# The first weight half by two DMA queues, and one zeroing matmul in bf16 in place of fp32

## The chip, the cores and the metric

The kernel runs on one core of a Trainium2 chip. The metric is the device time of one execution in us, as the median of several runs; the profiled span is some 1.8 us shorter.

## The reference

```python
def _attn_ref(x, f_logit, lower_bound):          # x, f_logit: (4, 6080, 256)
    sig = 1.0 / (1.0 + np.exp(-f_logit))
    f = lower_bound + (1.0 - lower_bound) * sig
    i = 1.0 - f
    for t in range(S):                           # S = 6080
        h = f[:, t] * h + i[:, t] * x[:, t]
        y[:, t] = h
    return y

def _moe_ref(x, w_in, w_out):                    # x: y as (24320, 256)
    h = x @ w_in                                 # w_in (256, 2048), w_out (2048, 256), float64
    g = h - np.tanh(h)
    return g @ w_out
```

## The kernel before

The tokens go in one block of 256 and 47 of 512. The weights come as 64-bit numbers and are turned into fp32 on the chip, in seven steps on DVE and ScalarE (`ce` to `cw`). The order of all work is a hand-made list of words. The start of the opening's list:

```python
before = """
    K1.7 W.0 df.0 ce.0 cr.0 dx.0 cm.0 tf.0 cx.0 W.1 cs.0 tx.0 sg0.0 cb.0 K1.4
    sg1.0 df.1 v0.0 f0.0 cw.0 f1.0 v1.0 dx.1 ce.1 tf.1 sc1.0 cx.1 sc0.0 W.2 cr.1
    cm.1 tx.1 sg1.1 cb.1 sg0.1 cs.1 F.0.0.0 f0.1 v1.1 f1.1 dx.2 v0.1 K1.4 cw.1
    t.0.0.0 sc0.1 q.0.0.0 F.0.0.1 w.0.0.0 W.3 sc1.1 cr.2 K1.2 a.0.0.0 t.0.0.1
    F.1.0.0 ...          # cut
    ... m13.2 K
    a.1.3.1 P1.2.0 ...   # cut
"""
```

`W.n` loads weights (`W.0` and `W.1` are halves of 512 KB), `df.j` and `dx.j` load f_logit and x of block j, `tf.j` and `tx.j` transpose them on TensorE, `sg` is the sigmoid, `sc` the scan over time on DVE. `F.j.u.s` are the first-layer products of the first two blocks. `K1.n` are n filler matmuls on zeros that keep TensorE busy. From block 2 on another scheme is used, in which products add to a bank that holds older sums; for its first use that bank is zeroed, by the word `K`:

```python
def fetch_half(u, s, raw, queue):
    src = moe_w_in.rearrange("(p k) (s u f) -> s u p k f", k=KC, s=2, u=NU)
    queue.dma_start(out=raw.rearrange("p (k f) -> p k f", k=KC), in_=src[s, u])

def keep_busy(n):                       # the word K1
    for _ in range(n):
        nc.tensor.matmul(busy[:], lhsT=zeros.bitcast(BF16)[:, 0:P],
                         rhs=zeros.bitcast(BF16)[:, 0:TB], start=True, stop=True, ...)

def clear_B():                          # the word K, once
    bank = ps_b.tile([P, 2, HB], FP32, name="B", tag="B")
    nc.tensor.matmul(bank[:], lhsT=zeros[:, 0:P], rhs=zeros[:], start=True, stop=True, ...)
...
nc.scalar.dma_start(out=lb[:], in_=lower_bound.rearrange("(p k) -> p k", k=KC))
```

Here P = 128, TB = 512, HB = 256 and KC = 2. The whole opening up to the first product of block 1 (`F.1.0.0`) takes 17.5 us.

## Time and profile before

| | kernel before |
|---|---|
| time, 3 runs | 2331.93, 2332.53, 2333.46 us |
| profiled run | 2331.1 us, span 2329.3 us |
| TensorE / DVE / ScalarE busy | 100% / 91% / 77% |
| first weight half landed | 4.78 us |
| x of block 1 issued, landed | 3.84, 11.53 us |
| first product `F.0.0.0` | 12.70 us |

The lines themselves stand in the prediction.

### The profile page before, as it was taken

The page shows a single profiled execution, that of the slowest core. Times are in us where ns is not written, and L with a number is a line of the kernel's source. Part 1 is how long each engine was busy: PE and PEld are TensorE (multiplying, and loading weights), DVE is VectorE, ACT ScalarE, POOL GpSimd, SP SyncE. Part 2 cuts the span into 40 slices and gives each one's busy share as a digit, 9 for nine tenths or more (in the row PEclk, how much of TensorE's full clock was granted, in tenths as well). Part 3 has the DMA queues.
Part 4 walks back from the last instruction along what each step waited for, and adds up shares of the span by engine and source line. Part 5 has one row for each costly group of instructions (what it writes and reads, how often), then busy time and mean ns, then how long its engine had stood idle before and what let it go on. Part 6 is the DMA issues. An engine that isn't in the chain of part 4 may idle for free.

```text
span 2329.3 us, 28648 instructions
## 1 busy us (share of the span) xinstructions
PE 2319.6 (100%) x10677; PEld 2025.2 (87%) x10677; DVE 2121.4 (91%) x2447; ACT 1801.1 (77%) x2686; POOL 0.7 (0%) x6
## 2 busy tenths in 40 slices
PE   9999999999999999999999999999999999999998
PEld 6888888888888888888888888888888888888887
DVE  8999899998999989999999999999899998999987
ACT  7677777777777777787777777777777777777775
POOL 0000000000000000000000000000000000000000
PEclk9999999999999999999999999999999999999999
DMA  6311211111111111112111121111211112111101
GB/s 172 64 24 32 42 37 28 28 35 39 37 28 28 37 36 37 28 28 42 32 37 28 28 45 28 37 28 28 46 29 36 28 28 46 31 33 28 28 10 29
DMA packets 296932, 85.05 MB, mean 37 GB/s; under 512 B 289872, under 2 KB 292688, under 8 KB 296784
## 3 DMA queue, kind: packets, MB, share of 16 engines
q1 hardware_dynamic: 296640, 83.14, 16.9%
q8 instruction: 85, 1.39, 0.2%
q14 instruction: 63, 0.52, 0.1%
q10 hardware_dynamic: 144, 0.00, 0.0%
HBM read 58.20 MB, written 24.90 MB: 36 GB/s over the span
## 4 chain that ended last, share of the span: by engine, by line
PE 99%; DMA 0%; SPq 0%; DVE 0%; issue 0%
PE A L383 27%; PE Qd L466 14%; PE Qa L466 14%; PE Qb L466 14%; PE D L383 14%; PE Qc L466 7%; PE B L383 7%; PE Qc L749 1%; PE Qb L749 1%; PE Qa L749 1%; PE A L682 1%; PE D L682 0%; PE Qd L682 0%; DMA xn<-in_x_dram 0%; PE B L682 0%; PE Qc L682 0%
## 5 line engine op out<-in xcount | busy, mean ns | idle before, releaser
L383 PE MATMUL A<-T,w_in 128*128 128x256 f32 x2208 | 558.8, 379 | 0.0
L383 PEld LDWEIGHTS A<-T,w_in 128*128 128x128 f32 x2208 | 419.5, 190 | 57.0
L427 DVE TENSOR_TENSOR h<-h,q 128x1024 f32<-128x1024 f32 x368 | 437.7, 1220 | 3.1
L421 DVE SCALAR_TENSOR_TENSOR q<-q,t 128x1024 f32<-128x1024 f32 x368 | 440.2, 1217 | 0.0
L414 ACT ACTIVATE q<-t 128x1024 f32<-128x1024 f32 x368 | 382.8, 1053 | 46.3 <-DVE h L427 43.4
L411 ACT ACTIVATE t<-h 128x1024 f32<-128x1024 f32 x368 | 388.7, 1057 | 3.1 <-DVE h L398 0.3
L432 ACT ACTIVATE junk<-t 128x1024 bf16<-128x1024 f32 x368 | 388.2, 1055 | 1.5
L446 DVE TENSOR_TENSOR Tg<-h 128x1024 f32<-128x1024 f32 x368 | 348.1, 946 | 6.4
L466 PE MATMUL Qb<-h,w_out 128*128 128x256 f32 x1472 | 347.7, 379 | 0.0
L466 PEld LDWEIGHTS Qb<-h,w_out 128*128 128x128 f32 x1472 | 279.7, 190 | 38.0
L466 PE MATMUL Qa<-Tg,w_out 128*128 128x256 f32 x736 | 219.0, 379 | 0.0
L466 PE MATMUL Qd<-h,w_out 128*128 128x256 f32 x736 | 219.0, 379 | 0.0
L466 PE MATMUL Qa<-h,w_out 128*128 128x256 f32 x736 | 218.9, 379 | 0.0
L466 PE MATMUL Qd<-Tg,w_out 128*128 128x256 f32 x736 | 218.9, 379 | 0.0
L395 ACT COPY h<-B 128x512 f32<-128x512 f32 x184 | 107.0, 582 | 143.2 <-PE B L383 94.4
L395 ACT COPY h<-A 128x512 f32<-128x512 f32 x184 | 107.3, 583 | 136.7 <-PE A L383 125.3
L398 DVE TENSOR_TENSOR h<-D,r 128x512 f32<-128x512 f32 x184 | 126.9, 690 | 92.9 <-PE D L383 90.8
L398 DVE TENSOR_TENSOR h<-A,r 128x512 f32<-128x512 f32 x184 | 126.3, 687 | 74.3 <-PE A L383 42.5
L395 ACT COPY r<-A 128x512 f32<-128x512 f32 x184 | 107.3, 583 | 105.9 <-PE A L383 105.9
L383 PE MATMUL D<-y,w_in 128*128 128x256 f32 x736 | 188.9, 379 | 0.0
L383 PE MATMUL B<-y,w_in 128*128 128x256 f32 x736 | 188.9, 379 | 0.0
L383 PE MATMUL A<-y,w_in 128*128 128x256 f32 x736 | 188.9, 379 | 0.0
(120 smaller groups left out, 3069.8 us busy)
## 6 DMA issues: line engine op xcount, KB each, us to landing
xn<-in_x_dram SPq DMA_DIRECT2D x184, 128.0 KB, 3.2
fn<-in_f_logit_dram SPq DMA_DIRECT2D x184, 128.0 KB, 3.1
out_dram<-osb SPq DMA_DIRECT2D x180, 128.0 KB, 2.8
raw<-in_moe_w_in_dram SPq DMA_DIRECT2D x8, 512.0 KB, 4.6
raw<-in_moe_w_out_dram SPq DMA_DIRECT2D x8, 512.0 KB, 4.8
out_dram<-osb SPq DMA_DIRECT2D x3, 256.0 KB, 3.7
fn<-in_f_logit_dram SPq DMA_DIRECT2D x1, 512.0 KB, 6.9
xn<-in_x_dram SPq DMA_DIRECT2D x1, 512.0 KB, 7.7
```

The costliest lines, as they stand in the source:

```text
L383: nc.tensor.matmul(ps[:, c], lhsT=w_in[u][:, slot, c * P : (c + 1) * P], rhs=mixes[j][right], start=start and c == 0, stop=True, skip_grou ...
L395: nc.scalar.copy(out=dst, in_=piece(n, bank))
L398: nc.vector.tensor_tensor(out=piece(n, "h")[:, q], in0=piece(n, bank), in1=piece(n, r), op=ALU.add)
L411: nc.scalar.activation(out=half(n, i, "t"), in_=half(n, i), func=AF.Square)
L414: nc.scalar.activation(out=half(n, i, "q"), in_=half(n, i, "t"), func=AF.Square, scale=RA, bias=RB,)
L421: nc.vector.scalar_tensor_tensor(out=q, in0=q, scalar=RC, in1=t, op0=ALU.add, op1=ALU.mult)
L427: nc.vector.tensor_tensor(out=h, in0=h, in1=q, op=ALU.mult)
L432: nc.scalar.activation(out=junk[:, :, :, 0 : st[n]["hb"]], in_=t, func=AF.Relu, bias=-TINY, accum_out=flags[:, 2 * n + i : 2 * n + i + 1],)
L446: nc.vector.tensor_tensor(out=o, in0=a, in1=b, op=ALU.subtract)
L466: nc.tensor.matmul(acc[j, part][:, r, 0 : st[n]["hb"]], lhsT=w_out[u][:, slot, c * P : (c + 1) * P], rhs=piece(n, right)[:, q, c], start=( ...
L682: nc.tensor.matmul(h[c], lhsT=w_in[u][:, 2 * k + s, c * P : (c + 1) * P], rhs=ys[j][:, k, 0:nb], start=k == 0 and (c == 0 or len(banks) == 2),
L749: nc.tensor.matmul(acc[j][i // 2][:, i % 2].rearrange("p (k m) -> p k m", k=2), lhsT=plain[j, u][:, s, c, i * P : (i + 1) * P], rhs=w_out[ ...
```

## The change

One intent is to have the first weights sooner, by issuing their two halves of the channels at once from SyncE and from ScalarE. The other is to make the one zeroing of the bank cheaper, since zeros are zeros in any type.

```diff
-    def fetch_half(u, s, raw, queue):
+    def fetch_half(u, s, raw, queues):
         src = moe_w_in.rearrange("(p k) (s u f) -> s u p k f", k=KC, s=2, u=NU)
-        queue.dma_start(out=raw.rearrange("p (k f) -> p k f", k=KC), in_=src[s, u])
+        dst = raw.rearrange("p (k f) -> p k f", k=KC)
+        n = KC // len(queues)
+        for i, queue in enumerate(queues):
+            part = slice(i * n, (i + 1) * n)
+            queue.dma_start(out=dst[:, part], in_=src[s, u][:, part])
...
-                fetch_half(u, order[i][2], raw[:], nc.sync)
+                queues = (nc.sync, nc.scalar) if i == 0 else (nc.sync,)
+                fetch_half(u, order[i][2], raw[:], queues)
...
-            K1.7 W.0 df.0 ce.0 ...
+            K1.7 df.0 ce.0 ...
...
             nc.tensor.matmul(
-                bank[:], lhsT=zeros[:, 0:P], rhs=zeros[:], start=True, stop=True,
+                bank[:], lhsT=zeros.bitcast(BF16)[:, 0:P],
+                rhs=zeros.bitcast(BF16)[:, 0:TB], start=True, stop=True,
...
+            open_by(["W.0"])
             nc.scalar.dma_start(
                 out=lb[:], in_=lower_bound.rearrange("(p k) -> p k", k=KC)
             )
```

More of the change, by code (lines that the diff above doesn't have):

```diff
@@ L803, in fast @@
         before = """
-            K1.7 W.0 df.0 ce.0 cr.0 dx.0 cm.0 tf.0 cx.0 W.1 cs.0 tx.0 sg0.0 cb.0 K1.4
+            K1.7 df.0 ce.0 cr.0 dx.0 cm.0 tf.0 cx.0 W.1 cs.0 tx.0 sg0.0 cb.0 K1.4
             sg1.0 df.1 v0.0 f0.0 cw.0 f1.0 v1.0 dx.1 ce.1 tf.1 sc1.0 cx.1 sc0.0 W.2 cr.1
```

## The prediction

> **What bounds the kernel now.** I read the page first. TensorE is busy for the whole span.
>
> ```profile
> span 2329.3 us, 28648 instructions
> PE 2319.6 (100%) x10677; PEld 2025.2 (87%) x10677; DVE 2121.4 (91%) x2447; ACT 1801.1 (77%) x2686; POOL 0.7 (0%) x6
> PE 99%; DMA 0%; SPq 0%; DVE 0%; issue 0%
> ```
>
> A busy TensorE can still hide waits, so I asked next for the waits of TensorE over the whole span. This is the complete list of its idle stretches over 0.15 us:
>
> ```profile
> PE Qa L627 <- DMA fn<-in_f_logit_dram: 1.9, 2, 1.0
> PE B L853 <- DVE ones L879: 1.5, 1, 1.5
> PE Qa L533 <- DVE C L526: 0.4, 1, 0.4
> PE Qc L627 <- DMA xn<-in_x_dram: 0.3, 1, 0.3
> ```
>
> The columns are total us, times, longest us. All but one (the 0.4 us on L533, at 2322 us) lie before 12.7 us. So the span has two parts. From 12.70 us to about 2322 us TensorE never stops, and a cost there counts only if it is TensorE time. Before 12.70 us TensorE waits for data, partly covered by filler matmuls on zeros (L853). To see what that opening waits for, I took the chain of waits of the first 30 us (start us, length us, what):
>
> ```profile
> 0.75 0.67 SPq L103
> ...
> 2.61 0.55 SPq L103
> 3.16 0.04 issue
> 3.20 0.60 SPq L613
> 3.80 0.04 issue
> 3.84 7.69 DMA xn<-in_x_dram
> 11.53 0.14 issue
> 11.67 0.71 PE Qc L627 x4
> 12.38 0.48 PE Qd L627 x4
> 12.86 1.73 PE A L682 x8
> 14.59 0.86 PE B L853 x4
> ```
>
> The item that ends the opening is the transfer of the second block of x: issued at 3.84 us, landed at 11.53 us, transposed by TensorE until 12.7 us. It is **not** the first weight half, which landed at 4.78 us (the conversion on DVE starts at 4.81 us, L134) and whose converted form was ready at 8.40 us (L128, 7.71 + 0.69), over 4 us before its first matmul.
>
> The x transfer takes 7.69 us because it stands behind others in one queue: 512 KB of weights, 256 KB of f_logit, 256 KB of x, 512 KB of weights and 512 KB of f_logit, then its own 512 KB, in all 2.62 MB. The windows of 0.25 us show how the DMA engines start up (the last two numbers are the DMA share and GB/s):
>
> ```profile
> 2.00:2.25 0.25, 0.25 (x2) 0.02 (x1) 0.00 (x0) 0.25 (x1) 0.00 (x0) 1.00 1.02 50
> 2.50:2.75 0.25, 0.25 (x2) 0.03 (x1) 0.00 (x0) 0.25 (x3) 0.00 (x0) 1.00 0.52 172
> 3.00:3.25 0.25, 0.25 (x2) 0.10 (x1) 0.00 (x0) 0.00 (x0) 0.00 (x0) 1.00 1.34 287
> 4.00:4.25 0.25, 0.25 (x2) 0.00 (x0) 0.00 (x0) 0.00 (x0) 0.00 (x0) 1.00 1.07 393
> ```
>
> From about 3.75 us on they run at 260 to 420 GB/s, mostly near 360. Between 2.0 and 3.75 us they ramp up: 50, 115, 172, 221, 287, 238 and 344 GB/s, which makes 0.36 MB where 360 GB/s would have moved 0.63 MB. The missing 0.27 MB are worth 0.27 / 0.36 = 0.76 us.
>
> **What the Trainium skill says.** "DMA: Bandwidth & Descriptors", section Issuing engines are not separate DMA queues, says that transfers started by different engines run on the same 16 DMA engines, and that issuing from several only saves the sequencer's time to start them. This case agrees as far as it goes: once the queue is full one queue alone holds the engines at a share of about 1.0. So I expect nothing from the split after 3.75 us; what it can change is the issue time and the ramp. "FP8 and Floating Point Precision", section TensorE Precision Notes, says that true FP32 takes four passes. The trace agrees: an f32 matmul of 512 columns from zeros shows as two records 0.429 us apart, so 0.858 us, while the warm bf16 fillers of 512 columns start every 0.216 us; the ratio is 4.0. "TensorE: Matmul & The Clock Gate", section Back-to-back issue gap, gives N/2.4 + 2.5 ns for a warm isolated matmul, 215.8 ns at 512; the trace has 215 to 216 ns.
>
> **Part 1, the bank zeroed in bf16.** It runs once, not once per block: the order of the work calls it one time, and the trace shows one fp32 matmul in two records.
>
> ```profile
> L863 PE MATMUL B<-zeros x2: 592/592/592, 84.6 to 85.1; 128*128 128x512 f32 x2
> ```
>
> In the timeline of TensorE the zeroing begins at 84.632 us, the next matmul (L383) at 85.490 us, and there is no idle on either side: 0.858 us of TensorE time. The changed kernel puts one bf16 matmul there, 0.216 us. Saved: 0.858 - 0.216 = **0.64 us**, in a place where TensorE is the bound. It is kept if the work behind it can come earlier by as much. The next product needs block data and weights that were made earlier. The one after next (B, 88.08 us) waits for the ScalarE copy that began at 86.55 us and took 0.57 us; that copy follows the product and moves with it. From 90 to 100 us DVE is busy 7.68 of 10 us, so it can follow. I count the whole 0.64 us.
>
> **Part 2, two queues for the first weights.** SyncE issues 256 KB instead of 512 KB; ScalarE issues the other 256 KB at the same moment, ahead of the 1 KB of lower bounds. Two gains follow. The first issue took 0.67 us; a half should take about 0.45 us (my estimate between 0.37 us, the issue of the lower bounds with as many rows, and 0.67), so all later SyncE issues come about 0.2 us earlier. And the ramp is fed from two sides, which I suppose to recover a third to a half of its 0.76 us. These are two views of the same start, so I do not add them: I take that the second x block lands **0.35 us** earlier, between 0 and 0.7. TensorE then starts its first real matmul at 12.35 instead of 12.70 us, and everything behind follows, because DVE too waits there (1.1 us idle at 12.97 us, released by the same transposes). What the part adds is about 0.4 us of issue on ScalarE before its table load, and a later landing of the lower bounds (2.49 us now, likely about 4 to 4.6 us, behind the half weight on that queue). Their two small activations need 0.2 us each and precede the conversion of the weights on ScalarE; the first consumer of their result on DVE is at 7.32 us. There is room, but not much before 6.38 us.
>
> **Sum.** 0.64 + 0.35 = 0.99 us of 2332.53 us, 0.04%: about **2331.5 us**.
>
> **Rivals.** (a) The opening gains nothing: the x transfer has the same 2.62 MB ahead of it or in it on the same 16 engines, and if the engines' own start rather than the queue causes the ramp, it lands at 11.5 us as before. For it: the share of about 1.0 from 3.75 us on. Then only 0.64 us is left: 2331.9 us. (b) A wait takes its place: ScalarE sits behind the late lower bounds, the first sigmoid slips beyond 6.38 us, and v and the scans of block 0 delay DVE. Against it: DVE has 1.1 us of slack at 12.97 us. Beyond that slack it would cost up to 0.5 us: 2332.4 us. (c) TensorE overtakes its feeders after 85 us and the 0.64 us come back as waits; for it: DVE is busy 9.86 and 9.93 of 10 us in the two windows from 100 to 120 us; against it: 8.82 of 10 in the next, and 91% overall. Then about 2332.1 us. (d) TensorE's clock. The transposes before 9.2 us run at half pace (0.213 us apart) and those after 10.2 us at full (0.120 us); if the earlier data move that change behind the first products, their 16 matmuls at 0.427 rather than 0.216 us would cost up to 3.4 us: 2335 us. I give it a few per cent, since more earlier work, not less, should reach it.
>
> **Range and chances.** The first three runs lie between 2331.93 and 2333.46 us, so the median itself is uncertain by about 0.5 us each time. With 0.3 us for the opening and 0.2 us for the zeroing the spread is some 0.7 us, and a range of 2330.4 to 2332.6 us should hold it 8 times in 10. A change of 2% is 47 us. The whole opening is 12.7 us long, so faster by 2% is out of reach, and slower by 2% needs a stall in every block, which nothing here touches: the order of instructions after the opening is the same on every engine.
>
> **What would show it right or wrong.** Right: one bf16 record of the zeroing, the next L383 matmul 0.216 us after it, no new idle of TensorE after 12.4 us; the second x block landing near 11.2 us; a first SyncE issue near 0.45 us; higher GB/s between 2.25 and 3.5 us. Wrong: x landing at 11.5 us or later (rival a), ScalarE idle on the lower bounds and a sigmoid after 6.4 us (b), waits of TensorE on DVE beyond 85 us (c), first products more than 0.22 us apart (d). A new wait in each block would break the whole reckoning.

## The result and the profile after

The changed kernel took 2331.0 us as the median of 6 runs (2330.37 to 2332.34), the kernel before 2332.3 us in 6 runs (2331.25 to 2333.46). The ratio is the mean time of one kernel's runs over that of the other's of the same rounds, so not quite the ratio of these medians: 0.9995, with a 95% interval of 0.9982 to 1.0008. That is inside the predicted range.

The profiled run is one of the slower ones (2331.9 us, span 2330.1 us), and its span is **longer** than the one of the kernel before (2329.3 us). This trace needs care. First the page, then all waits of TensorE (total us, times, longest us):

```profile
span 2330.1 us, 28649 instructions
PE 2318.8 (100%) x10676; PEld 2025.3 (87%) x10676; DVE 2121.3 (91%) x2447; ACT 1800.6 (77%) x2686; POOL 0.7 (0%) x6
```

```profile
PE Qa L632 <- ACT e L145: 2.4, 1, 2.4
PE B L858 <- DVE ones L885: 1.5, 1, 1.5
PE Qa L632 <- DMA fn<-in_f_logit_dram: 1.4, 1, 1.4
PE Qa L538 <- DVE C L531: 0.4, 1, 0.4
```

TensorE works 0.8 us less and still ends later, because it waits longer in the opening. The new 2.4 us before the transposes of block 1 are put down to ScalarE, but f_logit of block 1 landed only at 10.22 us and the transposes began at 10.35 us, so it is the transfer (0.13 us from landing to transpose, as before: 10.06 and 10.20 us). The chain of waits of the opening (start us, length us, what) shows what came of it:

```profile
0.75 0.40 SPq L107
...
11.81 1.10 PE Qc L632 x4
12.91 0.85 PE Qd L632 x4
13.76 2.20 PE A L687 x8
15.96 0.86 PE B L858 x4
```

Before, the same transposes took 0.71 and 0.48 us and the same eight products 1.73 us. x of block 1 landed at 11.67 us, 0.14 us later than before, and then the work itself was slow. The windows tell why (span of the window, busy times of the engines, then TensorE's clock, DMA share, GB/s):

```profile
2.00:2.25 0.25, 0.25 (x2) 0.02 (x1) 0.00 (x0) 0.25 (x1) 0.00 (x0) 1.00 0.71 147
2.50:2.75 0.25, 0.25 (x2) 0.03 (x1) 0.00 (x0) 0.25 (x1) 0.00 (x0) 1.00 0.75 221
...
4.00:4.25 0.25, 0.25 (x2) 0.00 (x0) 0.00 (x0) 0.00 (x0) 0.00 (x0) 1.00 1.02 353
7.77:11.18 3.41, 1.05 (x9) 0.86 (x8) 3.41 (x9) 1.84 (x4) 0.00 (x0) 1.00 1.06 357
11.18:14.59 3.41, 3.36 (x15) 2.81 (x14) 1.85 (x4) 2.42 (x4) 0.00 (x0) 0.50 1.23 269
```

The DMA engines move more in their first windows than before (147 for 50 GB/s, 221 for 172). But from 11.18 to 14.59 us TensorE has **half its clock**. In the kernel before the trace's clock record turns full at 9.32 us and stays so until the work ends. (The clock column means nothing before a trace's first clock record, at 4.35 us here: it prints 1.00 there, while the first fillers run at half pace, 0.427 us apart.) Finally the zeroing:

```profile
L868 PE MATMUL B<-zeros x1: 379/379/379, 86.0 to 86.0; 128*128 128x512 bf16 x1
```

It starts at 86.00 us and the next product at 86.22 us. If every matmul of the two traces is set beside its partner, the changed kernel is 1.37 us late from 14.7 us on, 0.73 us late after the zeroing, and stays so to its end. So this trace says: the zeroing saved 0.64 us, and this run's opening was 1.37 us longer. Is that the fault of the split, or of the run?

### The profile page after: what moved, and what is told of

The parts are those of the page before. It is cut to its first block, busy times and chain, and to the rows that moved or that the text cites. A ratio compares the mean times of both kernels' runs of the same rounds, so it can differ in the third digit from the quotient of the medians.

```text
span 2330.1 us, 28649 instructions
## 1 busy us (share of the span) xinstructions
PE 2318.8 (100%) x10676; PEld 2025.3 (87%) x10676; DVE 2121.3 (91%) x2447; ACT 1800.6 (77%) x2686; POOL 0.7 (0%) x6
## 4 chain that ended last, share of the span: by engine, by line
PE 99%; DMA 0%; DVE 0%; issue 0%; ACT 0%; SPq 0%
PE A L388 27%; PE Qd L471 14%; PE Qa L471 14%; PE D L388 14%; PE Qb L471 14%; PE B L388 7%; PE Qc L471 7%; PE A L687 1%; PE Qc L754 1%; PE Qa L754 1%; PE Qb L754 1%; PE D L687 0%; PE Qd L687 0%; PE B L687 0%; DMA fn<-in_f_logit_dram 0%; PE Qa L687 0%
## 5 line engine op out<-in xcount | busy, mean ns | idle before, releaser
L388 PE MATMUL D<-T,w_in 128*128 128x256 f32 x736 | 188.9, 379 | 0.0
```

The lines of the kernel that those rows point to most:

```text
L388: nc.tensor.matmul(ps[:, c], lhsT=w_in[u][:, slot, c * P : (c + 1) * P], rhs=mixes[j][right], start=start and c == 0, stop=True, skip_grou ...
```

## The experiments

**Theory A**: the zeroing is worth 0.64 us and the split next to nothing. **Theory B**, the prediction: the split also brings x of block 1 some 0.35 us earlier. **Theory C**: the clock lapse is an accident of the run, and explains both the spread of equal runs and the odd profile. Twelve kernels ran, three groups of four, each group on one chip beside 9 runs of the kernel before. All gave correct results.

The table has one trace for each kernel. "90%" and "last" are when 90% and 100% of the 1 KB packets of f_logit and x of blocks 0 and 1 had been moved, counted from the packet records of the trace. "To F" is the time from the landing of x to the first product of block 1 (`F.1.0.0`), "rest" from there to the end of TensorE's work, all in us.

| run | queues, zeroing | half clock after 11 us | 90% | last | x landed | to F | rest |
|---|---|---|---|---|---|---|---|
| before | one, fp32 | no | 9.83 | 11.03 | 11.53 | 5.92 | 2306.22 |
| after | two, bf16 | yes | 9.46 | 11.15 | 11.67 | 7.15 | 2305.58 |
| e1 | one, bf16 | yes | 9.94 | 11.44 | 11.95 | 7.50 | 2305.58 |
| e2 | two, fp32 | no | 9.53 | 10.65 | 11.16 | 5.92 | 2306.22 |
| e3 | two, bf16 | yes | 9.73 | 10.95 | 11.50 | 7.22 | 2305.58 |
| e4 | two, bf16, more fillers | no | 9.77 | 11.60 | 12.10 | 5.92 | 2305.58 |
| e5 | one, bf16, more fillers | no | 10.04 | 11.08 | 11.64 | 5.92 | 2305.58 |
| e6 | two, bf16, bounds first | yes | 9.68 | 11.34 | 11.86 | 7.39 | 2305.58 |
| e7 | two, bf16, no fillers | yes, until 15.91 | 9.72 | 11.68 | 12.19 | 7.65 | 2305.57 |
| e8 | one, fp32 21 times | yes | 10.04 | 11.59 | 12.10 | 7.52 | 2323.39 |
| e9 | one, bf16 | yes | 10.03 | 11.30 | 11.80 | 7.29 | 2305.58 |
| e10 | two, bf16 | no | 9.47 | 10.53 | 11.04 | 5.92 | 2305.58 |
| e11 | one, bf16, more fillers | no | 10.20 | 11.32 | 11.84 | 5.92 | 2305.58 |
| e12 | one, bf16, x ahead of weights | no | 8.93 | 10.94 | 11.50 | 5.05 | 2309.07 |

Times, as means in us:

| group | before (9 runs) | its four kernels (5 runs each) |
|---|---|---|
| 1 | 2332.29 | e1 2330.95, e2 2332.02, e3 2331.01, e4 2331.09 |
| 2 | 2331.98 | e5 2330.71, e6 2331.38, e7 2331.68, e8 2348.97 |
| 3 | 2332.01 | e9 2331.74, e10 2331.32, e11 2331.02, e12 2332.97 |

### e1, the zeroing alone

```diff
 # the kernel before, with the bf16 matmul in clear_B and nothing else
```

> The kernel before with the bf16 zeroing alone, one weight queue as before. Theory A (the zeroing is 0.64 us of TensorE time on the path, the queue split gives nothing or costs a little): 0.6 us below the kernel before, some 2331.7 us, and as fast as or faster than the changed kernel. Theory B (the split brings x earlier, as predicted): 0.6 us below before, but 0.35 us above the changed kernel. In both the zeroing is one record and the next product starts 0.216 us after it.

The mean fell by 1.34 us in a group where the single runs of one kernel spread over 2.4 to 2.8 us. The exact number is in the table: with fp32 the rest takes 2306.22 us, with bf16 2305.58 us, in every trace of that zeroing and order, whatever the opening was. The difference is **0.64 us**. This trace also has the clock lapse, with one queue, so the split does not cause it. Its chain of waits:

```profile
3.85 8.11 DMA xn<-in_x_dram
11.95 0.14 issue
12.09 1.10 PE Qc L627 x4
13.19 0.85 PE Qd L627 x4
14.04 2.55 PE A L682 x8
```

### e2, the split alone

```diff
 # the changed kernel, with the fp32 matmul in clear_B put back
```

> The changed kernel with the fp32 zeroing put back, so the queue split alone. Theory A: no gain over the kernel before (2332.3 us, within 0.3 us), the second x block lands at 11.5 to 11.7 us as before, the lower bounds land near 5.6 us and ScalarE waits for them. Theory B: 0.35 us below before, x landing near 11.2 us.

x landed at 11.16 us, which speaks for B; the mean is only 0.27 us below the kernel before, which speaks for neither. One trace was not enough, hence the repeats.

### e3 and e10, the changed kernel again

> The changed kernel once more, on the chip of the other runs, for the spread of its runs. Theory C (the time of one run depends on where TensorE's clock changes in the opening): again a spread of 1 to 2 us between equal runs, and in the trace either half-pace transposes and first products after 11 us (then the profiled run near 2332 us) or full pace there (near 2331 us). Against C: a spread like that with the same clock record each time.

> The changed kernel again, partner of the run with the zeroing alone. Theory A: x of the second block lands between 11.1 and 12.2 us as in all runs with one queue; Theory B: near 11.2 us. By the clock (theory C) its fastest runs are near 2330.2 to 2331.1 us with a recorded clock of 1.000, slower ones 1 to 2 us above.

e3 has the lapse (11.15 to 14.56 us), e10 has not: the same program, and both ways. e10 is how the opening looks when all goes well:

```profile
3.54 7.50 DMA xn<-in_x_dram
11.04 0.14 issue
11.17 0.71 PE Qc L632 x4
11.89 0.48 PE Qd L632 x4
12.37 1.73 PE A L687 x8
```

Compare the lengths with those of e1: 0.71 + 0.48 + 1.73 us against 1.10 + 0.85 + 2.55 us for the same work. It was also the run with the shortest span of its group (2328.4 us, 2330.19 us of time).

### e9, the zeroing alone again

```diff
 # the same kernel as e1, beside e10 on one chip
```

> The bf16 zeroing alone again (one weight queue, old fillers), beside the changed kernel on one chip. Theory A (the split gives nothing): median and mean within 0.4 us of the changed kernel's. Theory B (the split is worth 0.35 us or more): at least 0.35 us above it. The trace ends its products 2305.6 us after the first product of the second block in any case.

Mean 2331.74 us against 2331.32 us for e10: 0.42 us for the split, but only 0.11 us by the medians, so A and B are not told apart. In group 1 the same pair (e3 against e1) gave 0.06 us the other way. The three pairs (e2 against before, e3 against e1, e10 against e9) average to a gain of 0.21 us, with a scatter as large as that. A fourth pair, e4 and e5 below, lies on two chips: medians of 2330.72 us with the split and 2330.73 us without. (The record of the zeroing itself is missing from e9's trace; a gap of 0.22 us stands in its place.)

### e4, e5 and e11, more fillers

```diff
-            K1.7 df.0 ce.0 ... sg0.0 cb.0 K1.4
+            K1.11 df.0 ce.0 ... sg0.0 cb.0 K1.12
```

e4 is the changed kernel with this edit; e5 and e11 have one queue and the bf16 zeroing.

> The changed kernel with more filler matmuls: 11 in place of 7 before the first transposes and 12 in place of 4 before the second, so that TensorE is not idle long enough to lose its clock. Theory C: no half-clock record between 9 us and the end of the products, the first product near 12.85 us in place of 13.56 us, a spread below 0.7 us, and a median 0.3 to 0.8 us below the changed kernel. Rival to C (the clock makes no difference to the end, DVE sets the start of the products): the same median as the changed kernel within 0.2 us, or longer because the fillers delay the transposes.

> One weight queue, bf16 zeroing, and the 11 and 12 fillers: the partner of the run with fillers and the split, so that the two differ by the split alone and neither should lose the clock. Theory A (the split does not move x): median within 0.3 us of its partner (2330.7 us on the earlier chip). Theory B (the split is worth 0.35 us): 0.35 us above it. In the trace, the first quadrant product of the second block follows the landing of x by 5.9 us and the end of the products follows that by 2305.6 us, as in all warm runs so far.

> One queue, bf16 zeroing, 11 and 12 fillers again: the version that looks best so far. Theory C (fillers keep TensorE's clock): again no run above 2331.5 us, mean near 2330.7 us, 0.3 us or more below the mean of the changed kernel on the same chip. Against C: a spread of 2 us as in the kernels with the old fillers.

None of the three traces (nor e12, with the same fillers and six more) has a lapse; of the nine traces with the old fillers six have it. The ten runs of e5 and e11 all lie between 2330.23 and 2331.18 us, with a standard deviation of 0.29 us against 0.73 us for the changed kernel's 16 runs. Their mean, 2330.86 us, is 0.33 us (standard error 0.20 us) below that of the changed kernel (2331.19; on the one chip that they shared, e11 lies 0.30 us below e10) and 1.28 us below that of the kernel before (2332.14 in 33 runs). e4 kept its clock in the trace, but one of its runs took 2332.61 us, which no trace explains; its median was 0.39 us below e3's and its mean no lower, so for the split kernel the theory's promise of a small spread failed.

### e6, the lower bounds first

```diff
-            open_by(["W.0"])
             nc.scalar.dma_start(out=lb[:], ...)
+            open_by(["W.0"])
```

> The changed kernel with the lower bounds issued on the ScalarE queue ahead of the half weight. Theory A (their late landing is hidden by slack): the lower bounds land near 2.5 us in place of 5.65, ScalarE no longer waits 2.5 us for them, the sigmoid of block 0 starts 0.3 to 0.6 us earlier, and the time stays the same as that of the changed kernel (within 0.3 us), since x lands as before. Rival (their landing is on the path): 0.3 us or more below the changed kernel.

In the changed kernel ScalarE waits for the lower bounds, as its list of waits says:

```profile
ACT om L893 <- DMA lb<-in_lower_bound_dram: 2.5, 1, 2.5
```

In e6 they landed at 3.68 instead of 5.65 us (2.5 was expected), that wait shrank to 0.55 us, and the sigmoid started at 6.56 instead of 6.98 us. The time did not follow: 0.60 us below its before, where the changed kernel lies 0.69 to 1.28 us below. These means are too uncertain to show it, but nothing speaks for the late bounds being on the path: in e6 TensorE still waited 2.4 us for f_logit and 0.28 us for x.

### e7, no fillers

```diff
-            K1.7 df.0 ce.0 ... sg0.0 cb.0 K1.4
+            df.0 ce.0 ... sg0.0 cb.0
```

> The changed kernel without the 7 and 4 filler matmuls of the opening, so that TensorE's clock is at half when x lands. Theory C (the clock after x has landed is on the path): the clock record turns full only after 13 us, the 8 transposes cost 0.75 us more and the products of the first block 1 to 2.5 us more, and the median is 1.5 to 3.5 us above the changed kernel. Rival (DVE, which follows with conversions and scans, hides it): within 0.5 us of the changed kernel.

The trace did as theory C said: full clock only at 15.91 us and 7.65 us from landing to F. The time did not rise as much as expected. It lies 0.30 us below its before, where the changed kernel lies about 1.0 us below, so the loss is some 0.7 us. Part of the reason is that I compared with a kernel that loses its clock in many runs itself. Two runs at 2330.76 and 2331.24 us are too fast for a slow opening; what their clock did is not known.

### e8, the zeroing 21 times

```diff
+            for _ in range(21):
                 nc.tensor.matmul(
                     bank[:], lhsT=zeros[:, 0:P], rhs=zeros[:], start=True, stop=True,
```

> The kernel before with the fp32 zeroing of the bank done 21 times in a row in place of once (the result is the same). Theory A (every zeroing is TensorE time on the path, at 0.858 us each): 20 x 0.858 = 17.2 us above the kernel before, 2349 us. Rival (TensorE has slack there and part of it is hidden): clearly less than 17 us, and then the 0.64 us of the bf16 form would not be kept in full either.

```profile
L864 PE MATMUL B<-zeros x42: 592/592/593, 86.8 to 104.4; 128*128 128x512 f32 x42
```

The rest is 2323.39 - 2306.22 = 17.17 us longer, and the time 16.99 us. Forty more records at 0.429 us are 17.16 us. So each added zeroing is path in full; that the 0.64 us saved are kept in full is read from the rest in the table.

### e12, x ahead of the second weight half

```diff
-  ... cx.0 W.1 cs.0 ... dx.1 ce.1 tf.1 sc1.0 cx.1 sc0.0 W.2 cr.1 ...
+  ... cx.0 cs.0 ... dx.1 W.1 tf.1 sc1.0 sc0.0 W.2 ... F.0.0.0 ... sc0.1 sc1.1 cr.1 F.1.0.0 ce.1 ... cw.1 W.3 F.0.0.1
```

> The former with the second weight half issued behind the second block of x instead of ahead of it, and its conversion behind the scans. Theory D (x waits for the bytes ahead of it, not for the start of the queue): x lands 1.2 to 1.5 us earlier, near 10.3 us, because 0.52 MB fewer are ahead at some 360 GB/s. The product that starts the second block then starts about 2 us earlier, but DVE has to convert later, so the time falls by no more than 0.6 us. Rival to D (the transfer's own latency sets it): x lands at 11.5 us or later as before.

The fillers are those of e11, but for ten in place of four after `F.0.0.0` (not in the cut above). As "to F" and "rest" follow another order of work here, they don't compare with the other rows.

Theory D fell, as far as one trace shows. With 0.52 MB fewer ahead of it, 90% of the packets were through 1.27 us earlier than in e11 (8.93 against 10.20 us), but the last came at 10.94 against 11.32 us, and x landed at 11.50 against 11.84 us. The landing follows the **last** packet by 0.50 to 0.56 us in all 14 traces. In e12 between 9.5 and 11 us the 1 KB packets trickle at 31, 16 and 10 per half microsecond while weight packets already flow beside them: this looks as if most of the DMA engines were done with x and one or a few late ones held the landing. The packets take 46 ns each, so ten in 0.5 us are about the work of a single engine. The records name no engine, so this is inferred, and why one is late stays open. The kernel became slower (2332.97 us): the converted weights now came too late, and a new wait appeared in TensorE's list of waits:

```profile
PE B L682 <- DVE w_in L128: 1.3, 1, 1.3
```

### What follows for the split and for the clock

With one queue and the old place of x (before, e1, e5, e8, e9, e11) the 90% mark is at 10.01 us on average, with two (after, e2, e3, e4, e6, e7, e10) at 9.62 us: **0.39 us earlier**. By 4.0 us the DMA engines had moved 0.37 MB with one queue and 0.52 MB with two. The ramp is not steeper, though, it only begins earlier: the packet records give the first 0.02 MB at 2.57 us with one queue and 2.15 us with two, 0.5 MB at 4.37 and 3.95 us, 2.0 MB at 8.72 and 8.32 us (means of the same traces), so the lead is about 0.4 us from the first bytes on and does not grow. The changed kernel's windows from 1.75 us on (74, 147, 205, 221, 229, 279 and 344 GB/s) are nearly those of the kernel before from 2.00 us on (50, 115, 172, 221, 287, 238 and 344). Its size is that of the issue time saved: in the profile after the change the first issue was 0.27 us shorter, and the next five came 0.26 to 0.43 us sooner (that of x of block 1 at 3.52 instead of 3.84 us). But x landed at 11.81 us on average with one queue (11.53 to 12.10) and at 11.65 us with two (11.04 to 12.19): 0.16 us, with a standard error of about 0.18 us. The scatter of the last packets covers the gain.

For the clock its records tell. From x's landing to F takes 5.92 us in all six traces of the ordinary order without a lapse, and 7.15 to 7.52 us in the six with fillers and a lapse: **1.2 to 1.6 us**. As the same program gives both (e3 and e10), the lapse is not the program's alone. In the four lapses that I read in full (after, e1, e3, e9) a stretch of 1.9 to 2.4 us in which TensorE was idle went before. In e9 the windows before and within the lapse are:

```profile
4.51:7.92 3.41, 1.50 (x10) 1.23 (x10) 2.10 (x5) 2.06 (x5) 0.00 (x0) 1.00 1.03 347
7.92:11.33 3.41, 2.34 (x8) 1.18 (x7) 3.41 (x8) 1.79 (x4) 0.00 (x0) 0.50 1.08 365
```

The window ahead of the lapse was busy for 1.50 of 3.41 us there and for 1.05 us in the changed kernel's trace; in e11, which kept its clock, the busy time of two windows in a row was 3.08 and 3.01 us. The busy time of the window sorts all traces. Counted in steps of 3.41 us from a trace's first record of the full clock, the windows at full clock that a lapse followed were busy for 1.05 to 1.82 us (after, e1, e3, e6, e8, e9), and none of 2.06 us or more was followed by one. The nearest on each side are in e8, which lapsed at 12.42 us, and in the changed kernel's trace, which kept its clock at 7.77 us:

```profile
9.00:12.42 3.42, 1.82 (x11) 1.25 (x10) 3.33 (x7) 1.50 (x3) 0.00 (x0) 1.00 1.06 375
4.35:7.77 3.42, 2.06 (x13) 1.36 (x12) 1.94 (x4) 2.09 (x7) 0.00 (x0) 1.00 1.05 353
```

This also tells why the same fillers help in one run and not in another. Among the nine traces with the old fillers, where the clock turned full early, at 4.3 to 5.3 us (after, e1, e3, e6, e9), a lapse followed each time; where it turned full only at 9.0 to 10.1 us (before, e2, e8, e10), it followed in e8 alone. In the kernel before the four fillers after the first transposes ran at half pace and lasted 1.91 us, in the changed kernel's trace at full pace and 1.03 us, so they left TensorE idle for 0.86 and 2.36 us.

The lapse is not the whole spread either: x landed anywhere from 11.04 to 12.19 us in these traces, and that shifts the end as well.

The timed runs have no trace, but each has its mean recorded clock to three digits. 1.000 allows at most 2 x 0.0005 x 2330 = 2.3 us at half clock, so no lapse of 3.41 us. It is a rough sieve. The mean counts all before the first record as full (three of the five runs of e7 are at 1.000), and it counts the half clock after the work's end, so that 0.999 need not be a lapse (the traces of before, e2 and e10 have none and stand at 0.999). Among the 27 runs of the kernel before in the three groups, the 11 at 1.000 average 2331.34 us and the others 2332.61 us. Among the changed kernel's 16 runs the 9 at 1.000 average 2330.82 us. Like with like the change is worth 0.52 us, with a standard error of 0.19 us, which holds the 0.64 us of the zeroing alone. The larger step of the medians, 1.3 us, includes the draw: 4 of the 6 runs of the changed kernel were at 1.000. Whether the changed kernel lapses less often (9 of 16 at 1.000, against 11 of 27) is not settled.

## Why the prediction was right or wrong

- **The zeroing, 0.64 us**: right to the hundredth (2306.22 - 2305.58), right that it is kept in full (e8), right that it happens once.
- **The split, 0.35 us**: the mechanism was half right. The first issue took 0.40 us (0.45 estimated), and 90% of the packets came 0.39 us earlier. But "the ramp is fed from two sides", which was to recover a third to a half of its 0.76 us, is not seen: the ramp has the same slope and begins some 0.4 us earlier. The next step, "I take that the second x block lands **0.35 us** earlier", is not shown: it landed 0.16 +- 0.18 us earlier, so the term was too large or is lost in scatter.
- **"The x transfer takes 7.69 us because it stands behind others in one queue"**: not the sole cause, as far as one trace shows. e12 took 0.52 MB from ahead of it; 90% of the packets came 1.27 us earlier, but x itself only 0.34 us of the 1.4 us that 0.52 MB are at 0.36 MB per us. The landing hangs on the last packets, which neither an earlier start nor fewer bytes moved much.
- **Rival a**, nothing gained in the opening and 2331.9 us: not told apart from the split's estimate. All runs of the zeroing alone (e1 and e9) average 2331.35 us, those of the changed kernel 2331.19 us.
- **Rival b**, late lower bounds: they were later than I said (5.65 us, not 4 to 4.6), the sigmoid did slip to 6.98 us, and it cost nothing that e6 could recover. The slack of DVE seems to have taken it: DVE still sat idle for 1.56 us before its first work on block 1 (1.09 us before the change). I did not foresee that the next weight transfer would be held up (issued at 5.04 instead of 4.39 us, waiting for a first half to land); it was not needed soon, and nothing waited for it.
- **Rival c**, TensorE overtaking its feeders: did not happen; after the opening there is only the old 0.4 us wait.
- **Rival d**, the clock: I gave it "a few per cent", for a full clock that comes too late because of the change. What happened is another thing: the clock was full and was lost again. It comes with the old fillers in either kernel, in six of nine traces (three of four with one queue, three of five with two), and at 1.2 to 1.6 us it is larger than either part of the change. The cost was within my "up to 3.4 us", the frequency far above my guess.
- **My signs of being wrong**: in the profile after the change three of the four showed at once: x landed after 11.5 us (a), the sigmoid came after 6.4 us behind the lower bounds (b), and the first products ran at half clock (d). None of them tells what the split is worth; that took the repeats.
- **The sum**: 2331.5 us, measured 2331.0 us (2331.19 as the mean of 16 runs). The hit says little of its parts: the range was 2.2 us wide and held rival a's 2331.9 us too, and part of the larger step is luck, the draw of runs without a lapse. What the runs prove is the zeroing.

## What to carry to other kernels

When an engine has no idle time after its opening, a microsecond of its work anywhere is a microsecond of the span, and a trace shows it to a hundredth where timed runs cannot. Here a transfer landed 0.50 to 0.56 us after its last packet, and the last tenth of the packets trailed by 1.0 to 2.0 us, so an earlier start or a shorter queue helped less than its bytes suggest. Before comparing single profiles of a kernel with a short idle opening, look at TensorE's clock record, and add fillers until it holds: here that made ten runs agree within 1 us and, with the bf16 zeroing and one queue, gave the lowest mean, 2330.86 us (by less than two standard errors), so nothing here shows that the second queue is needed.

## What the Trainium skill lacked or had wrong

- "TensorE: Matmul & The Clock Gate", section What's actually happening, lists the half-rate state as the default and "after ≥1 idle window (~3.4µs)". It doesn't say how idle such a window has to be. Here it was not wholly idle: the clock halved after windows of 3.41 us in which TensorE was busy for 1.05 us (the changed kernel) to 1.82 us (e8), and held after all with 2.06 us or more. The window's length agrees: the lapses last 3.41 us or, in e9, twice that.
- "DMA: Bandwidth & Descriptors", section Issuing engines are not separate DMA queues, says that issuing from several engines only saves the sequencer's time. The traces agree: the issues came 0.26 to 0.43 us sooner and the bytes some 0.4 us sooner, with no steeper ramp. The section gives no figure for the saving; at the start of this kernel it meant 0.52 MB moved by 4.0 us in place of 0.37 MB.
- "DMA: Bandwidth & Descriptors", section Why a DMA increments its semaphore by 16 and not by 1, says that the engines of a transfer finish independently. It gives no size for it: here the last packet came 1.0 to 2.0 us after the 90% mark, which was more than the gain from 0.52 MB fewer ahead (0.34 us).
